# Another set of due times and engine choices for the jobs of an attention and gated-FFN kernel

## The chip, the cores and the metric

The program runs on one core of a Trainium2 chip. The metric is the device time of one execution in microseconds. Its engines have queues of their own: PE (TensorE: matmuls, with weight loads shown as PEld), DVE (VectorE), ACT (ScalarE), POOL (GpSimd) and SP (here only a queue that issues DMAs). Each queue runs strictly in the order in which its instructions were recorded, and an instruction waits on semaphores for what it reads or overwrites.

## The reference

Eight batches of eight heads, 576 positions, head size 64. Queries and keys are rotated, attention is computed per head, and the heads of a batch, laid side by side (512 channels), go through a gated block with a causal convolution of five taps.

```python
q_rot, k_rot = (rotate(q), rotate(k))
scores = scale * np.matmul(q_rot, k_rot.transpose(0, 1, 3, 2))
attn = np.exp(scores - max); attn = attn / (sum + 1e-09)
x = attn @ v                      # heads side by side: (8, 576, 512)
gate_pre += conv_w[k] * xp[:, k:k + S, :]          # k = 0..4
gate = 1.0 / (1.0 + np.exp(-gate_pre))
return gate * (x @ w_val) @ w_out
```

## The kernel before

The work is cut into 32 pairs of heads (p = 0 to 31), four pairs to a batch (b = 0 to 7). All products are float32 made of high and low parts (three products for one). The kernel records its work as some 3,400 jobs. A job has a name, a due time and an engine. The due time is a base written in the code plus an offset from the table DUE; the table PICK chooses the engine of the jobs that can run on more than one (V is DVE, A is ACT, G is POOL). `Plan.order` takes, of the jobs whose inputs were recorded and whose buffers are free, always the one with the smallest due time; this gives the order in every queue and also the rotation of the buffers. No due time is a time on the chip.

```python
            e = PICK.get(pick, e)
        plan.add(base + DUE.get(key, 0.0), e, fn, *args, r=r, w=w, port=port)
        heap = [(jobs[i][0], i) for i in range(len(jobs)) if not left[i]]
            i = heappop(heap)[1]
```

The jobs of one pair, with their names (a trailing e marks pairs 0 to 2, a trailing l the last pair or batch; `_0` and `_1` are the two column halves in which pair 0 is loaded and rotated):

- loadk, loadq, loadv: DMAs from SP (L198, L202). kmul0, kmul1, kadd, khi, klo and the same with q: the rotation and the split into high and low (L212, L216, L223, L227), on DVE, POOL and ACT. kfront and qmixed: small casts inside k, and of the last 64 query rows into a mixed tile (qm; L190 on ACT, L192 on DVE).
- s0 to s4: the scores (L255) of 128 query rows of both heads, s4 of the last 64 rows of both. They go to three PSUM banks. max0 to max8: row maxima on DVE (L261). exp0 to exp8: exponentials on ACT (L274), two to a score chunk; an exponential frees its bank.
- The probabilities are transposed. Pairs 3 to 30: x1, x3, x5, x7 turn 32x32 blocks on DVE (L289) and mv, 16 DMAs from SP (L294), put the blocks in place. Pairs 0 to 2 and 31: t0 to t7 and th on PE (L303, L316), with copies c0 to c7, ch1 and ch3 out of PSUM. tm, thm, cm, chm do this for the mixed rows.
- radd, rinv, rw, rr: reciprocal sums, written to DRAM and read back spread out. pv4, pv0, pv1: attention times v on PE (L359 to L377). norm0, norm1: DVE (L405).
- xhi, xlo: split of x (ACT L412, POOL L416). tap0 on ACT (L426), tap1 to tap4 on DVE (L429), gate on ACT (L433).

A batch whose four pairs are ready gives eight stage-0 groups f00 to f07 (four channel blocks by two column halves, 12 matmuls each, L463), each followed by a multiplication by the gate on DVE (L468), a high part on ACT (yh, L472) and a low part on POOL (yl, L476). Eight stage-1 groups f10 to f17 read these, go out through a copy on ACT or DVE (L482 on ACT) and a DMA from SP (L488). The groups of a batch lie between the scores of the pairs that come two to six places after its last one, in a pattern that repeats every four pairs.

The two weight matrices and the tap weights arrive as bits of 64-bit numbers. They are decoded in the head of the program: lval and lout load blocks (512 KB each, L527), dval and dout are six steps a block on DVE and ACT (L497 to L504), a cast (L534), a product on PE (L539 to L541) and a copy; dtap decodes the taps in seven instructions of 128x20 on DVE (L497 to L508). warm jobs are matmuls whose results nobody reads.

A POOL job that is recorded after a two-input DVE job waits for that DVE job by an added dependency (`self.behind`).

Of the kernel before, what the change touches and what calls it, by code (L numbers as in the profile page):

```python
# [144 lines left out]
def attn_gated_ffn(ctx: ExitStack, tc: tile.TileContext, q2, k2, v2, tab, w_val, conv_w, w_out, out, collect=None):  # L145
# [410 lines left out]
    def at(key, base, e, ns, fn, *args, pick=None, r="", w="", kb=0, mode=None, port=False):  # L556

        options = ns if pick else None
        if pick:
            e = PICK.get(pick, e)  # L560
            ns, port = options[e]
            args = [ENG[e] if a == "ENGINE" else a for a in args]
        plan.add(base + DUE.get(key, 0.0), e, fn, *args, r=r, w=w, port=port)
        if collect is not None:
# [244 lines left out]
```

## Time and profile before

| what | value |
|---|---|
| median of 3 runs | 650.75 us (646.76 to 650.79) |
| profiled execution | 650.38 us, its span 648.5 us |
| mean granted TensorE clock | 0.974 of full |
| busy, PE / DVE / ACT / POOL | 611.0 / 571.2 / 463.6 / 404.6 us |
| DMA | 139.16 MB, mean 215 GB/s |

The span is the time from the first to the last instruction; the execution has 1.9 us more around it. A busy PE counts matmuls at whatever clock was granted. The profile shows each instruction with the line of the kernel that recorded it, and the idle time before it with what ended it.

### The profile page before, as it was taken

The numbers are of one execution on the slowest core, as the hardware profiler recorded it, in microseconds if no ns is written. First come the engines' busy times: TensorE is split into PE (matmuls) and PEld (weight loads), VectorE is DVE, ScalarE is ACT, GpSimd is POOL, SyncE is SP. The second block draws the span as 40 slices with busy tenths as digits, with TensorE's granted clock in tenths as the row PEclk, the third lists the DMA queues.
The fourth block names the chain that finished last, engine by engine and source line by source line (L and its number), as shares of the span: only waits on it lengthen the run. The fifth ranks groups of instructions, "written<-read, shape, count | busy, mean of one in ns | idle before, by whom it ended". The sixth has DMA issues, their size and how long they took to land.

```text
span 648.5 us, 15339 instructions
## 1 busy us (share of the span) xinstructions
PE 611.0 (94%) x5611; PEld 500.6 (77%) x5611; DVE 571.2 (88%) x819; ACT 463.6 (71%) x1145; POOL 404.6 (62%) x309
## 2 busy tenths in 40 slices
PE   8898786899999999999999999999999999999997
PEld 8665554588878887888778887788788878888797
DVE  4999988899999999999999999999999998994532
ACT  3887866767777777876877777777877687776432
POOL 3324566678687869777778868776877777630200
PEclk9899976889999999999999999999999998999999
DMA  6634227888899899998999989999999889774011
GB/s 221 243 108 165 81 95 190 234 232 235 249 264 277 241 266 261 249 271 222 261 264 264 259 239 270 252 255 260 253 268 264 226 244 275 203 182 114 29 56 47
DMA packets 53019, 139.16 MB, mean 215 GB/s; under 512 B 11440, under 2 KB 21456, under 8 KB 52944
## 3 DMA queue, kind: packets, MB, share of 16 engines
q1 hardware_dynamic: 52400, 137.58, 75.4%
q8 instruction: 45, 0.74, 0.5%
q10 hardware_dynamic: 544, 0.59, 0.3%
q14 instruction: 30, 0.25, 0.1%
HBM read 62.48 MB, written 9.59 MB: 111 GB/s over the span
## 4 chain that ended last, share of the span: by engine, by line
PE 65%; DVE 11%; DMA 7%; POOL 5%; ACT 4%; issue 3%; SPq 3%; ACTq 0%; DVEq 0%; POOLq 0%
PE ps_t L463 23%; PE ps_s L255 16%; PE ps_t L369 14%; DVE nm L261 4%; DMA big<-big 3%; DVE big L289 3%; SPq L294 3%; PE ps_t L359 3%; PE ps_t L303 2%; DMA iq<-in_q 2%; PE ps_t L374 2%; DMA v<-in_v 2%; ACT p L274 2%; PE ps_t L330 2%; POOL yl L476 2%
## 5 line engine op out<-in xcount | busy, mean ns | idle before, releaser
L261 DVE TENSOR_REDUCE nm<-ps_s 128x1 f32<-128x576 f32 x288 | 204.6, 746 | 24.0 <-PE ps_s L255 23.8
L274 ACT ACTIVATE p<-ps_s,nm 128x576 f32<-128x576 f32 x256 | 188.3, 739 | 47.5 <-DVE nm L261 46.0
L255 PE MATMUL ps_s<-k,q 64*128 64x288 f32 x1536 | 146.9, 317 | 13.3 <-ACT p L274 9.7
L289 DVE STREAM_TRANSPOSE big<-p 128x1152 f32<-128x1152 f32 x112 | 150.9, 1361 | 0.0
L255 PEld LDWEIGHTS ps_s<-k,q 64*128 64x128 f32 x1536 | 112.7, 190 | 38.9 <-ACT p L274 19.9
L369 PE MATMUL ps_t<-big,v 128*64 128x256 f32 (+2 forms) x1024 | 119.4, 385 | 0.0
L429 DVE SCALAR_TENSOR_TENSOR g<-x,cw,g 128x576 f32<-128x576 f32 (+1 forms) x132 | 111.0, 843 | 1.5 <-ACT g L426 1.2
L212 POOL TENSOR_TENSOR iq<-iq,tab 128x576 f32<-128x576 f32 (+1 forms) x61 | 86.4, 1436 | 40.9 <-DVE g L429 8.9
L369 PEld LDWEIGHTS ps_t<-big,v 128*64 128x64 f32 x1024 | 70.8, 138 | 46.3 <-issue 15.6
L463 PE MATMUL ps_t<-yl,wout_hi 128*128 128x288 f32 x256 | 77.3, 302 | 4.9 <-POOL yl L476 4.9
L463 PE MATMUL ps_t<-xh,wval_hi 128*128 128x288 f32 x256 | 79.4, 310 | 0.0
L463 PE MATMUL ps_t<-yh,wout_hi 128*128 128x288 f32 x256 | 79.3, 310 | 0.0
L476 POOL TENSOR_TENSOR yl<-g,yh 128x288 fp32r<-128x288 f32 x56 | 48.8, 872 | 48.2 <-ACT yh L472 48.2
L227 POOL TENSOR_TENSOR q<-iq,q 128x576 fp32r<-128x576 f32 (+2 forms) x33 | 56.9, 1725 | 34.5 <-ACT q L223 30.6
L463 PE MATMUL ps_t<-xl,wval_hi 128*128 128x288 f32 x256 | 76.5, 299 | 0.0
L463 PE MATMUL ps_t<-xh,wval_lo 128*128 128x288 f32 x256 | 75.9, 296 | 0.0
L463 PE MATMUL ps_t<-yh,wout_lo 128*128 128x288 f32 x256 | 75.7, 296 | 0.0
L216 POOL TENSOR_TENSOR iq<-iq 128x576 f32<-128x576 f32 (+1 forms) x30 | 41.7, 1388 | 49.5 <-DVE g L429 43.2
L416 POOL TENSOR_TENSOR xl<-x,xh 128x576 fp32r<-128x576 f32 (+1 forms) x33 | 46.7, 1415 | 29.3 <-ACT xh L412 12.4
L463 PEld LDWEIGHTS ps_t<-yl,wout_hi 128*128 128x128 f32 x256 | 48.5, 189 | 7.3 <-POOL yl L476 6.3
L227 POOL TENSOR_TENSOR k<-ik,k 128x576 fp32r<-128x576 f32 x29 | 41.5, 1430 | 17.0 <-ACT k L223 5.3
L463 PEld LDWEIGHTS ps_t<-xh,wval_hi 128*128 128x128 f32 x256 | 49.3, 193 | 2.8 <-issue 2.6
(94 smaller groups left out, 1068.1 us busy)
## 6 DMA issues: line engine op xcount, KB each, us to landing
big<-big SPq DMA_DIRECT2D x448, 144.0 KB
ik<-in_k SPq DMA_DIRECT2D x31, 576.0 KB
iq<-in_q SPq DMA_DIRECT2D x31, 576.0 KB
v<-in_v SPq DMA_DIRECT2D x32, 320.0 KB
rb<-rd SPq DMA_DIRECT2D x64, 144.0 KB
out_t<-oo SPq DMA_DIRECT2D x64, 144.0 KB
big<-in_w_val SPq DMA_DIRECT2D x4, 512.0 KB
big<-in_w_out SPq DMA_DIRECT2D x4, 512.0 KB
```

Source lines behind the costliest of these rows:

```text
L212: eng.tensor_tensor(out=t[:, i, a:b], in0=t[:, i, a:b], in1=tabs[:, i, a:b], op=ALU.mult)
L216: eng.tensor_tensor(out=t[:, 0], in0=t[:, 0], in1=t[:, 1], op=ALU.add)
L227: eng.tensor_tensor(out=t[:, 1], in0=state[p][n + "in"][:, 0, a:b], in1=t[:, 0].bitcast(F32), op=ALU.subtract)
L255: T.matmul(out=ps[:, half, 0:288], lhsT=st["q"][rows, x, c * 128:c * 128 + 128] if c < 4 else mixq[p % 2][:, x], rhs=st["k"][rows, y, k0:k ...
L261: V.tensor_reduce(out=st[f"nm{i}"], in_=st[f"s{i}"], axis=AX.XY, op=ALU.max, negate=True)
L274: A.activation(out=pd.rearrange("p (b x) -> p b x", b=2), in_=st[f"s{i}"], func=AF.Exp, bias=st[f"nm{i}"], scale=1.0, accum_out=sums[p % 2 ...
L289: V.transpose(out=t[:, :, cs.index(c)].rearrange("p b k i -> p k b i"), in_=st[f"p{c}"].rearrange("p h s -> p (h s)").rearrange("p (k b i) ...
L369: T.matmul(out=acc[HEAD[h], 0:n], lhsT=st["v"][:, j, h, :], rhs=st["pt"][:, :, c0:c1, 5 * place(p, 2 * c0 + h) + j].rearrange("p a c i -> ...
L416: eng.tensor_tensor(out=st["xl"][:, a:b], in0=xs[p % 2][:, 4 + a:4 + b], in1=st["xh"][:, a:b].bitcast(F32), op=ALU.subtract)
L429: V.scalar_tensor_tensor(out=g, in0=x_sb[:, a + k:b + k], scalar=w, in1=g, op0=ALU.mult, op1=ALU.add)
L463: T.matmul(out=acc[:, 0:n], lhsT=wt[w][:, kc, ds], rhs=mv, start=(kc == 0 and i == 0), stop=(kc == NCH - 1 and i == 2))
L476: eng.tensor_tensor(out=ffn[b, "l", dc, lo], in0=y, in1=ffn[b, "h", dc, lo].bitcast(F32), op=ALU.subtract)
```

## The change

Only the two tables change. All 267 offsets of DUE have other values, so the order moves in every queue; 17 entries of PICK name another engine. No job is added, removed or altered, and DMAs are the same in number and size.

```diff
-DUE = {'taps': -9055.1904, 'dtap': 20.813, 'warm0': -111.0282, 'ltab_1': -9993.2863,
+DUE = {'taps': -8955.8597, 'dtap': -84.1915, 'warm0': -295.132, 'ltab_1': -9988.1565,
...
-PICK = {'c0': 'A', 'c0e': 'A', 'c1': 'A', 'c1e': 'A', 'c2': 'A', 'c2e': 'A', 'c3': 'V',
+PICK = {'c0': 'A', 'c0e': 'A', 'c1': 'V', 'c1e': 'A', 'c2': 'A', 'c2e': 'A', 'c3': 'A',
...
```

The 17 entries: from V to A qmixede and c3; from A to V ch3e, c1, c5, od1l and od2l; from G to V kmul0e, kmul1_0, qadd_0, qlo_0 and qlo_1; from V to G kmul1e, kadd_1, klo_0, kmul1_1 and qmul0_1.

What this does, first on DVE at the first pair, from its first two row maxima on (nm is written by a maximum, qm by a qmixed cast, L192 without qm is a copy of ch or c, 128x512 instructions on big are weight decoding). Before:

```order
L261 TENSOR_REDUCE nm_243<-ps_s_206 128x1
L261 TENSOR_REDUCE nm_270<-ps_s_205 128x1
L192 COPY qm_73<-q_71 64x2x64 x2
L261 TENSOR_REDUCE nm_278<-ps_s_254 128x1
L212 TENSOR_TENSOR ik_195<-ik_195,tab 128x576
L497 TENSOR_SCALAR big_234<-big_234 128x512
L261 TENSOR_REDUCE nm_292<-ps_s_255 128x1
```

Now the same place of DVE:

```order
L261 TENSOR_REDUCE nm_255<-ps_s_224 128x1
L261 TENSOR_REDUCE nm_274<-ps_s_225 128x1
L212 TENSOR_TENSOR ik_215<-ik_215,tab 128x576
L261 TENSOR_REDUCE nm_287<-ps_s_259 128x1
L261 TENSOR_REDUCE nm_291<-ps_s_260 128x1
```

The casts have left DVE (they are on ACT), and nothing stands between the third and the fourth maximum. The seven decoding steps of the taps, which stood among the work of pair 1, now stand on DVE ahead of the first scores. On SP a 512 KB block of w_val now stands between the first two loads and the other two loads of pair 0.

Second, DVE where pair 3 passes to pair 4 (x is L289; L429 are taps). Before, from max7 of pair 3 to max1 of pair 4:

```order
L261 TENSOR_REDUCE nm_1129<-ps_s_1116 128x1
L261 TENSOR_REDUCE nm_1133<-ps_s_1115 128x1
L289 STREAM_TRANSPOSE big_1034<-p_1101 128x9x4x32
L289 STREAM_TRANSPOSE big_1034<-p_1131 128x9x4x32
L429 SCALAR_TENSOR_TENSOR g_1071<-x_84,cw,g_1071 128x576
L429 SCALAR_TENSOR_TENSOR g_851<-x_85,cw,g_851 128x576
L261 TENSOR_REDUCE nm_1169<-ps_s_1162 128x1
L429 SCALAR_TENSOR_TENSOR g_1071<-x_84,cw,g_1071 128x576
L261 TENSOR_REDUCE nm_1188<-ps_s_1171 128x1
L261 TENSOR_REDUCE nm_1197<-ps_s_1172 128x1
```

Now, from max6 of pair 3 to max1 of pair 4:

```order
L261 TENSOR_REDUCE nm_1130<-ps_s_1116 128x1
L261 TENSOR_REDUCE nm_1132<-ps_s_1117 128x1
L502 SCALAR_TENSOR_TENSOR big_739<-big_739 128x512
L289 STREAM_TRANSPOSE big_1036<-p_1100 128x9x4x32
L503 TENSOR_SCALAR big_739<-big_739 128x512
L289 STREAM_TRANSPOSE big_1036<-p_1134 128x9x4x32
L429 SCALAR_TENSOR_TENSOR g_931<-x_85,cw,g_931 128x576
L504 SCALAR_TENSOR_TENSOR wout_lo<-big_739 128x512
L429 SCALAR_TENSOR_TENSOR g_1111<-x_84,cw,g_1111 128x576 x2
L261 TENSOR_REDUCE nm_1186<-ps_s_1172 128x1
L261 TENSOR_REDUCE nm_1190<-ps_s_1165 128x1
L261 TENSOR_REDUCE nm_1203<-ps_s_1173 128x1
```

The last steps of the last weight block moved behind the maxima of pair 3, and max8 of pair 3 behind max0 of pair 4; on PE the product of that block moved from ahead of s4 of pair 3 to between s0 and s1 of pair 4.

Third, DVE in the repeating pattern, where f06 and f05 of batch 1 are multiplied by the gate (L468). Before:

```order
L468 SCALAR_TENSOR_TENSOR g_2177<-g_2177,ps_t_3261 128x288
L429 SCALAR_TENSOR_TENSOR g_3241<-x_84,cw,g_3241 128x576
L261 TENSOR_REDUCE nm_3302<-ps_s_3289 128x1
L261 TENSOR_REDUCE nm_3304<-ps_s_3288 128x1
L468 SCALAR_TENSOR_TENSOR g_1919<-g_1919,ps_t_3314 128x288
L289 STREAM_TRANSPOSE big_3274<-p_3254 128x9x4x32
L429 SCALAR_TENSOR_TENSOR g_3241<-x_84,cw,g_3241 128x576
```

Now:

```order
L468 SCALAR_TENSOR_TENSOR g_2162<-g_2162,ps_t_3250 128x288
L429 SCALAR_TENSOR_TENSOR g_3226<-x_84,cw,g_3226 128x576
L261 TENSOR_REDUCE nm_3327<-ps_s_3283 128x1
L261 TENSOR_REDUCE nm_3331<-ps_s_3284 128x1
L289 STREAM_TRANSPOSE big_3270<-p_3265 128x9x4x32
L468 SCALAR_TENSOR_TENSOR g_1904<-g_1904,ps_t_3310 128x288
L429 SCALAR_TENSOR_TENSOR g_3226<-x_84,cw,g_3226 128x576
```

The multiplication for f05 moved behind a turn; on ACT its high part moved behind the second exponential of the chunk and kfront, where it stood between the two exponentials. On POOL the order there is unchanged. Elsewhere in the repeating pattern max8 stands behind max0 of the next pair, pv1 ahead of pv0, loadv behind rr, and single groups f trade places with their neighbours. In the last batch the two column halves trade places, the first half is now done first.

## Rows read from the trace of the kernel before

**Rows 1.** Windows: length, busy us (count) of PE, PEld, DVE, ACT, POOL; clock, DMA, GB/s
```profile
0.00:14.00 14.00, 11.98 (x82) 11.44 (x83) 5.85 (x17) 4.53 (x8) 3.88 (x10) 1.00 0.72 254
14.00:128.00 114.00, 94.54 (x722) 65.37 (x722) 101.62 (x159) 83.97 (x199) 55.79 (x39) 0.88 0.49 154
104.00:118.00 14.00, 12.28 (x62) 9.33 (x66) 11.20 (x14) 9.26 (x24) 10.03 (x7) 0.50 0.86 247
128.00:575.00 447.00, 436.82 (x4222) 364.38 (x4224) 430.61 (x587) 343.50 (x864) 336.96 (x253) 0.99 0.91 251
575.00:612.00 37.00, 35.50 (x353) 27.57 (x350) 20.14 (x34) 20.46 (x49) 6.33 (x6) 1.00 0.41 106
```

**Rows 2.** Timeline of PE, start and length in us, idle before and its releaser: pairs 3 to 4
```profile
102.60 0.61 PE L255 MATMUL ps_s<-k,q 64*128 64x288 f32 x1 [3.53 <-ACT pm L274]
```

**Rows 3.** Timeline of DVE, pairs 3 to 5
```profile
96.95 2.63 DVE L289 STREAM_TRANSPOSE big<-p 128x1152 f32<-128x1152 f32 x2
...
100.93 0.75 DVE L261 TENSOR_REDUCE nm<-ps_s 128x1 f32<-128x576 f32 x1
...
102.32 1.41 DVE L261 TENSOR_REDUCE nm<-ps_s 128x1 f32<-128x576 f32 x2
...
109.31 1.42 DVE L261 TENSOR_REDUCE nm<-ps_s 128x1 f32<-128x576 f32 x2 [1.00 <-PE ps_s L255]
...
113.57 1.42 DVE L261 TENSOR_REDUCE nm<-ps_s 128x1 f32<-128x576 f32 x2 [1.55 <-PE ps_s L255]
...
123.36 0.49 DVE L405 TENSOR_TENSOR x<-ps_t,rb 128x320 f32<-128x320 f32 x1 [1.40 <-PE ps_t L377]
```

**Rows 4.** Timeline of DVE, pairs 0 to 2
```profile
15.67 1.67 DVE L192 CAST qm<-q 64x128 fp32r<-64x128 f32 x2
17.45 0.76 DVE L261 TENSOR_REDUCE nm<-ps_s 128x1 f32<-128x576 f32 x1
18.24 0.76 DVE L212 TENSOR_TENSOR ik<-ik,tab 128x576 f32<-128x576 f32 x1
...
32.09 0.45 DVE L192 CAST qm<-q 64x128 fp32r<-64x128 f32 x2
...
53.19 1.49 DVE L192 CAST qm<-q 64x128 fp32r<-64x128 f32 x1
```

**Rows 5.** DVE by line and form: count, busy us, mean ns
```profile
L192 DVE COPY big<-ps_t 128x256 f32<-128x256 f32 x5 | 2.1, 420 | 1.4 <-PE ps_t L316 1.4
...
L499 DVE SCALAR_TENSOR_TENSOR oo<-oo,oo 128x20 int32<-128x20 int32 x1 | 0.2, 168 | 0.0
```

**Rows 6.** Timeline of POOL at the cast of pair 2
```profile
53.18 1.42 POOL L212 TENSOR_TENSOR iq<-iq,tab 128x576 f32<-128x576 f32 x1 [6.00 <-DVE wval_lo L504]
```

**Rows 7.** Timeline of PE, the stalls in the pattern of batch 0 and batch 1
```profile
182.68 1.05 PE L255 MATMUL ps_s<-k,q 64*128 64x288 f32 x11 [0.60 <-ACT p L274]
...
252.54 1.05 PE L255 MATMUL ps_s<-k,q 64*128 64x288 f32 x11 [0.60 <-ACT p L274]
...
255.13 0.40 PE L463 MATMUL ps_t<-yl,wout_hi 128*128 128x288 f32 x1 [0.82 <-POOL yl L476]
```

**Rows 8.** Timeline of DVE, the same place
```profile
251.66 0.45 DVE L468 SCALAR_TENSOR_TENSOR g<-g,ps_t 128x288 f32<-128x288 f32 x1
252.03 1.37 DVE L289 STREAM_TRANSPOSE big<-p 128x1152 f32<-128x1152 f32 x1
253.32 1.10 DVE L429 SCALAR_TENSOR_TENSOR g<-x,cw,g 128x576 f32<-128x576 f32 x1
```

**Rows 9.** Timeline of ACT, the same place
```profile
252.38 0.43 ACT L472 CAST yh<-g 128x288 fp32r<-128x288 f32 x1
...
253.43 0.30 ACT L190 CAST k<-k 128x128 fp32r<-128x128 f32 x1
```

**Rows 10.** Timeline of POOL, the same place
```profile
252.38 1.43 POOL L416 TENSOR_TENSOR xl<-x,xh 128x576 fp32r<-128x576 f32 x1
253.76 1.32 POOL L476 TENSOR_TENSOR yl<-g,yh 128x288 fp32r<-128x288 f32 x1
```

More of the change, by code (lines that the diff above doesn't have):

```diff
@@ L36 @@
-PICK = {'c0': 'A', 'c0e': 'A', 'c1': 'A', 'c1e': 'A', 'c2': 'A', 'c2e': 'A', 'c3': 'V', 'c3e': 'A', 'c4': 'A', 'c4e': 'A', 'c5': 'A', 'c5e': 'A', 'c6': 'A', 'c6e': 'A', 'c7': 'V', 'c7e': 'V', 'ch0': 'A', 'ch0e': 'V', 'ch1': 'V', 'ch1e': 'V', 'chm': 'A', 'chme': 'A', 'cm': 'A', 'cme': 'A', 'kadd': 'G', 'kadd_0': 'V', 'kadd_1': 'V', 'kadde': 'V', 'kfront': 'A', 'kfronte': 'A', 'klo': 'G', 'klo_0': 'V', 'klo_1': 'V', 'kloe': 'V', 'kmul0': 'G', 'kmul0_0': 'V', 'kmul0_1': 'V', 'kmul0e': 'G', 'kmul1': 'V', 'kmul1_0': 'G', 'kmul1_1': 'V', 'kmul1e': 'V', 'od0': 'A', 'od0l': 'A', 'od1': 'A', 'od1l': 'A', 'od2': 'A', 'od2l': 'A', 'od3': 'A', 'od3l': 'A', 'qadd': 'G', 'qadd_0': 'G', 'qadd_1': 'V', 'qadde': 'V', 'qlo': 'G', 'qlo_0': 'G', 'qlo_1': 'G', 'qloe': 'G', 'qmixed': 'A', 'qmixede': 'V', 'qmul0': 'G', 'qmul0_0': 'V', 'qmul0_1': 'V', 'qmul0e': 'G', 'qmul1': 'G', 'qmul1_0': 'G', 'qmul1_1': 'V', 'qmul1e': 'V', 'xlo': 'G', 'xloe': 'G', 'xlol0': 'G', 'xlol1': 'G', 'ylo': 'G', 'ylol': 'V', 'ch3': 'V', 'ch3e': 'A', 'decout': 'A', 'decval': 'A', 'odma': 'SP', 'odmal': 'SP', 'loadk': 'SP', 'loadk_0': 'SP', 'loadk_1': 'SP', 'loadke': 'SP', 'loadq': 'SP', 'loadq_0': 'SP', 'loadq_1': 'SP', 'loadqe': 'SP', 'loadv': 'SP', 'loadve': 'SP', 'mv0': 'SP', 'mv1': 'SP', 'mv2': 'SP', 'mv3': 'SP', 'rr': 'SP', 'rre': 'SP', 'rw': 'SP', 'rwe': 'SP'}
@@ new lines @@
+PICK = {'c0': 'A', 'c0e': 'A', 'c1': 'V', 'c1e': 'A', 'c2': 'A', 'c2e': 'A', 'c3': 'A', 'c3e': 'A', 'c4': 'A', 'c4e': 'A', 'c5': 'V', 'c5e': 'A', 'c6': 'A', 'c6e': 'A', 'c7': 'V', 'c7e': 'V', 'ch0': 'A', 'ch0e': 'V', 'ch1': 'V', 'ch1e': 'V', 'chm': 'A', 'chme': 'A', 'cm': 'A', 'cme': 'A', 'kadd': 'G', 'kadd_0': 'V', 'kadd_1': 'G', 'kadde': 'V', 'kfront': 'A', 'kfronte': 'A', 'klo': 'G', 'klo_0': 'G', 'klo_1': 'V', 'kloe': 'V', 'kmul0': 'G', 'kmul0_0': 'V', 'kmul0_1': 'V', 'kmul0e': 'V', 'kmul1': 'V', 'kmul1_0': 'V', 'kmul1_1': 'G', 'kmul1e': 'G', 'od0': 'A', 'od0l': 'A', 'od1': 'A', 'od1l': 'V', 'od2': 'A', 'od2l': 'V', 'od3': 'A', 'od3l': 'A', 'qadd': 'G', 'qadd_0': 'V', 'qadd_1': 'V', 'qadde': 'V', 'qlo': 'G', 'qlo_0': 'V', 'qlo_1': 'V', 'qloe': 'G', 'qmixed': 'A', 'qmixede': 'A', 'qmul0': 'G', 'qmul0_0': 'V', 'qmul0_1': 'G', 'qmul0e': 'G', 'qmul1': 'G', 'qmul1_0': 'G', 'qmul1_1': 'V', 'qmul1e': 'V', 'xlo': 'G', 'xloe': 'G', 'xlol0': 'G', 'xlol1': 'G', 'ylo': 'G', 'ylol': 'V', 'ch3': 'V', 'ch3e': 'V', 'decout': 'A', 'decval': 'A', 'odma': 'SP', 'odmal': 'SP', 'loadk': 'SP', 'loadk_0': 'SP', 'loadk_1': 'SP', 'loadke': 'SP', 'loadq': 'SP', 'loadq_0': 'SP', 'loadq_1': 'SP', 'loadqe': 'SP', 'loadv': 'SP', 'loadve': 'SP', 'mv0': 'SP', 'mv1': 'SP', 'mv2': 'SP', 'mv3': 'SP', 'rr': 'SP', 'rre': 'SP', 'rw': 'SP', 'rwe': 'SP'}
```

2 lines of the change are left out of this document (1 added, 1 removed).

## The prediction

> **What bounds the kernel now.** I read the table of busy time by stage first [rows 1]. From 128 to 575 us PE is busy 436.82 of 447 us: there TensorE is the bound, and DVE, busy 430.61 us, stands close behind. The pattern comes back after 69.9 us (252.54 - 182.68), and PE's timeline has only two gaps in each of its six passages: 0.60 us before a score chunk, which waits for an exponential to free its bank, and 0.82 us inside group f16, which waits for a low part from POOL [rows 7]. Six times 1.42 us is 8.5 of the 10.2 us that PE is idle in this stage. Nothing that only rearranges other engines can gain more than that here.
>
> From 14 to 128 us it is the other way round. PE is idle for 19.5 of 114 us and runs at a mean clock of 0.88, while DVE is busy 101.62 us, or 0.89 of the time [rows 1]. DVE has the weight decoding beside its maxima there, so what is taken off DVE in this stretch counts nearly in full, and 12.4 us of waiting is the most that a better order alone can win. The worst place is where pair 3 passes to pair 4: PE waits 3.53 us for the exponential that frees a bank [rows 2], and from 104 to 118 us its granted clock is 0.50, the lower level of 1.2 GHz [rows 1]. DVE then waits three times for the slow PE, 1.00, 1.55 and 1.40 us [rows 3]. Before the end, from 575 to 612 us, PE is idle 1.5 us [rows 1].
>
> The sum is made against the profiled execution, 650.38 us (span 648.5 us and 1.9 us around it). It lies 0.4 us under the median of the three runs, so the two can be used alike.
>
> **The change part by part.**
>
> *DVE work in the head.* The qmixed casts leave DVE for ACT, which has 30 us free in the stretch [rows 1]. Those of pair 1 cost 0.45 us and the long one of pair 2 1.49 us [rows 4]: together 1.94 us. Those of pair 0 cost 1.67 us, but the maximum behind them started at 17.45 only because PE had then just finished its scores, so I count them at nothing; that cover is worth up to 1.67 us if the scores come earlier. The copy ch3 comes to DVE three times, at 0.42 us each [rows 5]: 1.26 us added. The seven steps of dtap, 0.17 us each [rows 5], leave the full stretch for the time before the first scores, when DVE is busy 5.85 of 14 us [rows 1]: 1.18 us less. kmul0 and kmul1 of pairs 1 and 2 only trade engines. In all 1.94 - 1.26 + 1.18 = 1.86 us less, times 0.89 is **-1.7 us**. Bounds: nothing (all of it turns into waiting) and -3.5 us (with pair 0's casts).
>
> The long cast ran for 1.49 us while a POOL multiplication started 0.01 us before it and took 1.42 us [rows 4, 6]; the short pair beside an idle POOL took 0.45 us. The Trainium skill (SBUF — State Buffer, section Who interferes with whom) says that a DVE cast in its two-port mode and a GpSimd instruction exclude each other for the whole instruction, and that ACT waits for neither. These rows agree. By that rule the cast's whole 1.49 us go, since on ACT nothing locks it out, and the term is -1.7 us; without it the wait could pass to DVE's next instruction, only 0.45 us of pair 2's cast would go, and the term would be (0.90 - 1.26 + 1.18) x 0.89 = -0.7 us.
>
> *The first pair.* DVE's multiplication of 0.76 us that stood ahead of the fourth maximum [rows 4] moves to a place where DVE waits for PE's scores: -0.8 us. Against it, the first scores, which start shortly before 14 us, stand behind the taps and behind a load order in which a 512 KB block comes before half of pair 0. At 254 GB/s [rows 1] that block is 2.1 us. The delayed halves are needed last, behind the rotation of the first ones, so I take most of the 2.1 us as hidden and add 0.3 us (bounds -0.4, one DVE instruction of the rotation, and +1.2, all seven taps). Net **-0.5 us**.
>
> *Pair 3 to pair 4.* Weight steps move behind pair 3's maxima, so s0 of pair 4 can start earlier. But s1 of pair 4 needs two banks, those of max8 of pair 3 and of max0 of pair 4 and their exponentials. Before, max8 ran at 100.93 and the second tap and max0 after it [rows 3]; now the tap and max0 stand ahead of max8. The same instructions lie ahead of the second bank in both orders, so s1 starts when it did: **0 us**. In the hole that this leaves stands one weight product of PE. Bounds: -3.5 us (the hole closes) and +1.4 us (the two maxima once more).
>
> *The repeating pattern.* PE's order is the same but for pv1 ahead of pv0 and neighbours among the f groups, with equal work between the waits; loadv behind rr has a whole pair's time, a quarter of the 69.9 us, before it is read, and I cost both at nothing. The one place that touches a stall is f05. Its multiplication started at 251.66, behind it the turn, which took 1.29 us to the next start [rows 8]. Now it is behind the turn: it starts at 252.95 and ends at 253.40. The high part followed it on ACT at 252.38 [rows 9]; now both exponentials and kfront come first, and kfront, which ended at 253.73 with the high part's 0.32 us ahead of it, ends at 253.41. So the high part runs from 253.41 to 253.84, and the low part starts at about 253.9 instead of 253.76, when POOL was done with xl [rows 10]. Nearly all of the delay was covered by POOL. Six times 0.15 us is **+0.9 us**; bounds 0 and the rival below. The 0.60 us stall stays, since the first of the two exponentials still follows xhi.
>
> *The tail.* Copies c1 and c5 to DVE, c3 to ACT, od1l and od2l to DVE, the other column half first. PE's queue holds the same matmuls, and 1.5 us of waits are all there is to win or to shift: **0 us**, bounds -1.5 and +1.5.
>
> Sum: 650.4 - 1.7 - 0.5 + 0 + 0.9 + 0 = 649.1, say **649 us**.
>
> **The rivals.**
>
> A, *the clock is kept in the head*. If the weight product between s0 and s1 of pair 4 ends PE's wait in time, the 14 us at clock 0.50 don't come, and DVE's three waits for a slow PE, 3.95 us, go: 649.1 - 3.95 = 645 us. With half of DVE's other waits of the stretch (12.4 - 3.95, halved, is 4.2) it would be 641 us. For it: PE has one more piece of work in that place and s0 earlier. Against it: the piece itself waits for weight steps that now stand behind two turns on DVE.
>
> B, *f05 is late on POOL*, slower than before. Its place is the low part that f16 reads; the price is the whole delay of the turn, 1.29 us, in each of six batches, 7.7 us instead of 0.9: 649.1 + 6.8 = 656 us. It decides from the point at which POOL, done with xl at 253.76, waits for the high part longer than a tenth or two. For it: three things were put ahead, and the tap of DVE that stands beside the low part shows both instructions lengthened, 1.10 and 1.32 us [rows 8, 10]. Against it: POOL's own queue covered almost all of the delay in the working above.
>
> C, *the head's savings turn into waits*: DVE gets done earlier and waits for PE or ACT instead, as it already does for 12.4 us. Then only the 0.9 us remain: 651.3 us.
>
> **How the numbers follow.** The forecast has a chance of 0.45, A 0.20, B 0.15, C 0.20. The range goes from 641 (A with the halved waits) to 656 us (B), and leaves about 2 in 10 outside. One per cent, 6.5 us, is about what a measurement of this kernel can tell from no change. Under 644.2 us lie half of A and what the bounds of the forecast allow, 0.19; over 657.3 us lies the upper part of B and a head with a second stretch at the lower clock, 0.11; 0.70 are left for a change within 1%.
>
> **What the profile after would show.** Two PE gaps in each passage of the pattern as before, the one in f16 between 0.8 and 1.1 us: right for the pattern. DVE busy about 99 to 100 us in the stretch that ends with the first f04, and that stretch shorter by 2 us: right for the head. PE's gap before s1 of pair 4 cut in two by a weight product, with a clock of 0.5 behind it: right for that place. It is wrong if the period of a batch, 69.9 us, has changed by more than 0.3 us, if the clock in the head stays at its upper level (2.4 GHz) or falls in other places for long, or if a transfer, most of all the early 512 KB block, ends a wait on the path.

## The result: 1.0% slower

The changed kernel takes 653.09 us (median of 12, 651.40 to 657.49), the kernel before 647.24 us in the same comparison (median of 12, 643.92 to 650.79). The ratio is 1.0101, 95% interval 1.0071 to 1.0131. Ratios leave out executions that took over 1.5% longer than the fastest of their kernel; in e15 below these are two of twelve, at 660 us. I had forecast 649 us from a profiled execution of 650.38 us, so 1.3 us faster; measured is 5.9 us slower. That 653 us still lies between 641 and 656 us is in part luck: the execution that I started from took 3.1 us more than the median of before here.

The profiled execution after has a span of 651.2 us (652.97 us in all). In that of before the fourth period has a wait for a transfer (70.86 instead of 69.86 us), the clock fell behind its last pattern stall (1.45 us, see the end), and 4.4 us lie behind its last matmul where other kernels with that end have 3.3 to 3.7. By stages, with these three (1.0, 1.45 and about 1.1 us) taken out: the first stall of the pattern came 0.7 us later, the five periods between the first stall and the last took 355.94 instead of 349.3 us (**+6.6 us**), and the rest 111.85 instead of 112.9 us (-1.1): +6.2 us, close to the measured +5.9.

The table by stage, after (columns as in [rows 1]):

```profile
0.00:14.00 14.00, 8.48 (x54) 8.24 (x55) 7.43 (x21) 3.99 (x7) 4.42 (x10) 0.89 0.82 291
14.00:128.00 114.00, 98.70 (x751) 68.48 (x749) 101.29 (x152) 84.93 (x203) 55.39 (x39) 0.87 0.50 153
104.00:118.00 14.00, 12.57 (x64) 8.76 (x64) 11.45 (x15) 8.73 (x24) 10.66 (x8) 0.50 0.78 226
128.00:575.00 447.00, 432.49 (x4181) 355.11 (x4182) 432.54 (x580) 331.92 (x855) 335.75 (x251) 0.99 0.93 249
575.00:612.00 37.00, 36.46 (x348) 29.82 (x346) 24.09 (x39) 22.20 (x55) 7.74 (x8) 1.00 0.46 123
```

Against [rows 1] PE did 4.2 us more work in the stretch from 14 to 128 us, but this is work that it had not done by 14 us: from 0 to 128 us both kernels do 803 matmuls. From 128 to 575 us it lost 4.3 us of work, and DVE became busier by 1.9 us. What holds PE up there is in its table of waits (us in total, times, longest):

```profile
PE ps_t L463 <- POOL yl L476: 4.9, 6, 0.8
PE ps_s L255 <- ACT p L274: 4.5, 7, 0.9
PE ps_t L345 <- DVE pm L386: 2.7, 9, 0.5
PE ps_t L359 <- DMA big<-big: 1.8, 3, 0.8
PE ps_t L359 <- DMA ik<-in_k: 0.6, 1, 0.6
```

The first two are the old stalls of [rows 7] and the last waits ahead of the pattern, nearly unchanged. The last three, 5.1 us, are new but for 0.4 us: thm waits for the reciprocal sums of DVE, and pv4 for moved blocks of the turned probabilities. Why DVE is late is seen where f03 and f07 of batch 2 are multiplied. Before, DVE and then POOL (idle time and releaser in brackets):

```profile
297.16 0.81 DVE L429 SCALAR_TENSOR_TENSOR g<-x,cw,g 128x576 f32<-128x576 f32 x1
```

```profile
293.64 0.81 POOL L476 TENSOR_TENSOR yl<-g,yh 128x288 fp32r<-128x288 f32 x1
295.21 1.42 POOL L216 TENSOR_TENSOR iq<-iq 128x576 f32<-128x576 f32 x1 [0.76 <-DVE g L429]
```

After, DVE, then POOL, then PE's first matmul behind it:

```profile
295.83 1.22 DVE L429 SCALAR_TENSOR_TENSOR g<-x,cw,g 128x576 f32<-128x576 f32 x1
296.97 2.07 DVE L261 TENSOR_REDUCE nm<-ps_s 128x1 f32<-128x576 f32 x3
298.97 1.48 DVE L429 SCALAR_TENSOR_TENSOR g<-x,cw,g 128x576 f32<-128x576 f32 x1
301.78 0.20 DVE L386 RECIPROCAL pm<-sums 128x9 f32<-128x9 f32 x1
```

```profile
296.40 2.07 POOL L476 TENSOR_TENSOR yl<-g,yh 128x288 fp32r<-128x288 f32 x2
298.43 1.41 POOL L216 TENSOR_TENSOR iq<-iq 128x576 f32<-128x576 f32 x1
...
310.04 1.43 POOL L212 TENSOR_TENSOR iq<-iq,tab 128x576 f32<-128x576 f32 x1 [2.62 <-DMA iq<-in_q]
```

```profile
302.12 0.30 PE L345 MATMUL ps_t<-ident,pm 128*128 128x128 f32 x1 [0.30 <-DVE pm L386]
```

qadd (298.43 to 299.84) was running when tap4 came at 298.97; the tap ended 0.61 us after qadd and took 1.48 us where this tap took 0.81 before. qadd was that late because two low parts (f03 and f07) stand ahead of it now, where before only f03 did; the section on the change doesn't name this trade. Three maxima beside the same POOL work took 2.07 us, as in e15 below. The reciprocal ends at 301.98, and PE has waited 0.30 us. The late qadd also delays qlo, and with it, so I read it, the buffer for the next q: POOL then waited 2.62 us for its load, 9.7 us in 9 such waits from 128 to 575 us (2.8 us in 2 before).

### The profile page after: what moved, and what is told of

The parts are those of the page before. It is cut to its first block, busy times and chain, and to the rows that moved or that the text cites. A ratio compares the mean times of both kernels' runs of the same rounds, so it can differ in the third digit from the quotient of the medians.

```text
span 651.2 us, 15347 instructions
## 1 busy us (share of the span) xinstructions
PE 612.0 (94%) x5611; PEld 495.6 (76%) x5611; DVE 581.2 (89%) x821; ACT 453.5 (70%) x1143; POOL 407.4 (63%) x309
## 4 chain that ended last, share of the span: by engine, by line
PE 60%; DVE 16%; DMA 11%; ACT 5%; issue 3%; SPq 3%; POOL 1%; DVEq 0%; ACTq 0%
PE ps_t L463 23%; PE ps_s L255 15%; PE ps_t L369 11%; DMA big<-big 7%; DVE nm L261 5%; DVE big L289 5%; DVE g L429 3%; DMA ik<-in_k 3%; PE ps_t L359 2%; SPq L294 2%; ACT p L274 2%; PE ps_t L303 2%; PE ps_t L330 2%; PE ps_t L374 1%; PE ps_t L439 1%
## 5 line engine op out<-in xcount | busy, mean ns | idle before, releaser
L289 DVE STREAM_TRANSPOSE big<-p 128x1152 f32<-128x1152 f32 x112 | 151.7, 1362 | 0.0
L255 PEld LDWEIGHTS ps_s<-k,q 64*128 64x128 f32 x1536 | 112.9, 190 | 46.0 <-ACT p L274 22.3
L429 DVE SCALAR_TENSOR_TENSOR g<-x,cw,g 128x576 f32<-128x576 f32 (+1 forms) x132 | 126.1, 956 | 0.4
L369 PE MATMUL ps_t<-big,v 128*64 128x256 f32 (+2 forms) x1024 | 124.6, 386 | 0.0
L212 POOL TENSOR_TENSOR iq<-iq,tab 128x576 f32<-128x576 f32 (+2 forms) x62 | 88.6, 1443 | 46.2 <-DMA iq<-in_q 14.2
L369 PEld LDWEIGHTS ps_t<-big,v 128*64 128x64 f32 x1024 | 68.4, 138 | 41.1 <-issue 14.7
L476 POOL TENSOR_TENSOR yl<-g,yh 128x288 fp32r<-128x288 f32 x56 | 54.7, 982 | 44.0 <-ACT yh L472 43.5
L227 POOL TENSOR_TENSOR q<-iq,q 128x576 fp32r<-128x576 f32 x31 | 48.7, 1571 | 44.3 <-ACT q L223 42.7
L416 POOL TENSOR_TENSOR xl<-x,xh 128x576 fp32r<-128x576 f32 (+1 forms) x33 | 48.9, 1482 | 37.6 <-ACT xh L412 19.6
L216 POOL TENSOR_TENSOR iq<-iq 128x576 f32<-128x576 f32 x29 | 40.9, 1409 | 28.4 <-DVE g L429 26.2
L227 POOL TENSOR_TENSOR k<-ik,k 128x576 fp32r<-128x576 f32 (+1 forms) x30 | 42.6, 1419 | 18.5 <-DVE g L429 9.7
L463 PEld LDWEIGHTS ps_t<-yh,wout_hi 128*128 128x128 f32 x256 | 48.7, 190 | 2.6 <-issue 1.3
```

The costliest lines, as they stand in the source:

```text
L212: eng.tensor_tensor(out=t[:, i, a:b], in0=t[:, i, a:b], in1=tabs[:, i, a:b], op=ALU.mult)
L216: eng.tensor_tensor(out=t[:, 0], in0=t[:, 0], in1=t[:, 1], op=ALU.add)
L227: eng.tensor_tensor(out=t[:, 1], in0=state[p][n + "in"][:, 0, a:b], in1=t[:, 0].bitcast(F32), op=ALU.subtract)
L255: T.matmul(out=ps[:, half, 0:288], lhsT=st["q"][rows, x, c * 128:c * 128 + 128] if c < 4 else mixq[p % 2][:, x], rhs=st["k"][rows, y, k0:k ...
L289: V.transpose(out=t[:, :, cs.index(c)].rearrange("p b k i -> p k b i"), in_=st[f"p{c}"].rearrange("p h s -> p (h s)").rearrange("p (k b i) ...
L369: T.matmul(out=acc[HEAD[h], 0:n], lhsT=st["v"][:, j, h, :], rhs=st["pt"][:, :, c0:c1, 5 * place(p, 2 * c0 + h) + j].rearrange("p a c i -> ...
```

## The experiments

All times are medians, all ratios are against the kernel before on the same chip, with 95% intervals. Where a table is edited, P are the 84 offsets of pairs 3 to 30 and of the groups of batches 0 to 6, H the 131 offsets of pairs 0 to 2, the weights and the start, L the 52 of the last pair and batch.

**Parts alone (e1, e2, e3, e11, e12, e18).** Each takes the named parts of both tables from the changed kernel, the rest stays as before:

```diff
 e1: P    e2, e11: H    e3: L    e12: H and P    e18: H and L
-DUE = {... the part, before ...}
+DUE = {... the part, after ...}
```

> Only the offsets of the pairs 3 to 30 and of the groups of batches 0 to 6 are those of the changed kernel; head and last batch keep the old ones. Theory 1 (the loss is in the repeating pattern: the six periods of the profile after are 71.2 instead of 69.9 us, +5.6 us in all): slower than before by 5 to 8 us, ratio 1.008 to 1.012, since the gain of 3.7 us behind the last pattern stall is not in it. Theory 2 (the head sets the pace, and the pattern only inherits a worse start): within 1.5 us of before.

> Only the offsets and engines of pairs 0 to 2 and of the decoding of the weights are those of the changed kernel. Theory 1: the trace after reaches the first pattern stall 0.7 us later than before, so +0.7 us (0 to +1.5), and the period is 69.9 us as before. Theory 2: slower by 4 us or more, with longer periods although the pattern is the old one.

> Only the offsets and engines of the last pair and the last batch are those of the changed kernel. Theory 1: the part behind the last pattern stall, 111.85 instead of 115.5 us, shortens by up to 3.7 us: between -3.7 and 0 against before. Rival (that shorter end is only the other side of a longer pattern, work done already while the pattern waited): within 1 us of before.

> The kernel with only the head of the changed kernel, once more, for a profile (its 11 timed executions gave 653.7 us, 6 us over before). If the head itself is slow, the first stall of the pattern comes at 186 to 189 us instead of 182.7. If it comes within 1 us of 182.7, the loss lies behind it, in the pattern or at the end, though their orders are those of before.

> The changed kernel with the old order in the last pair and the last batch. If the shorter end of the changed kernel (111.9 against 115.5 us behind the last stall) comes from its own last batch, this is slower than the changed kernel by 3 to 8 us (119.7 us was measured there with the new pattern and the old end): 656 to 661 us. If the end follows from the pattern, it is the same as the changed kernel, 653 us.

> Head and last batch of the changed kernel with the old pattern. If the losses of the parts add up, head alone (+6 us) and last batch alone (+7 us) make it 13 us slower than before: 660 us, and the changed pattern, which then brings 653 us, is a gain beside these two. If the pattern is the loss of the change, this is 3 us or less slower than before.

| kernel | us | ratio |
|---|---|---|
| e1 P | 666.46 | 1.0284 (1.0226 to 1.0342) |
| e2 H | 653.67 | 1.0092 (1.0058 to 1.0127) |
| e3 L | 655.01 | 1.0087 (1.0051 to 1.0123) |
| e12 H, P | 659.49 | 1.0192 (1.0159 to 1.0226) |
| e18 H, L | 659.63 | 1.0171 (1.0126 to 1.0216) |
| after: H, P, L | 653.09 | 1.0101 (1.0071 to 1.0131) |

None of the parts is free. H and L add up (0.9 and 0.9 against 1.7% in e18), P does not: the three single losses make 4.6%, the whole loses 1.0%. The last batch costs 0.9% beside the old pattern and gives 0.9% back beside the new one (1.0192 to 1.0101). e1 lost 18.8 us, far over the 5 to 8 us expected; its pattern took 357.29 us between its first and last stall, as theory 1 says (8.0 us more), and the rest lies ahead of it and behind it. By parts the answer differs from that by stages: beside the changed head and last batch, the changed pattern is a gain of 0.7 points (1.0171 to 1.0101), as the expectation of e18 says for that result. It loses its 6.6 us between the stalls, but with the old pattern the first stall came at 188.34 instead of 183.41 us and the rest behind the last stall took 118.4 instead of 111.85 us. So "the pattern is the loss" holds for the stage and not for the part. e11 is e2 once more, for its trace: 653.27 us, first stall at 185.09 us, 2.4 us later than in [rows 7]; of the five periods behind it, two were at the old 69.86 us, in two the clock fell, and the last took 70.57.

**The taps' order alone (e4).**

```diff
-'kmul1': 18.3059, 'tap4': 36.7731, 'norm0': 26.8498, 'norm1': 25.9637,
+'kmul1': 17.6557, 'tap4': 35.5325, 'norm0': 19.9937, 'norm1': 3.084,
 (and x1 to x7, vz, pv, xhi, tap0 to tap3 and gate as after)
```

> In the pattern only the offsets of taps, gate, norms, turns, xhi and kmul1 are those of the changed kernel (maxima, exponentials, POOL, SP and groups as before). On DVE the last tap now stands ahead of kmul1 and the norms of the older pair trade places. Theory 1a (the taps now meet POOL's instructions, both lengthened, and DVE, already busy 430.61 of 447 us, becomes the bound): the mean tap grows from 864 towards 956 ns and the time by 3 to 7 us. Rival 1b (the maxima and exponentials are the cause: max8 behind max0 of the next pair delays radd and rinv): within 1.5 us of before. Rival 1c (loads and moves from SP land late): within 1.5 us of before.

704.55 us, 1.0855 (1.0797 to 1.0912), far over the 3 to 7 us expected. In this mix tap4 follows the first maximum directly. DVE, then POOL, in one pair:

```profile
257.00 0.75 DVE L261 TENSOR_REDUCE nm<-ps_s 128x1 f32<-128x576 f32 x1
257.67 1.60 DVE L429 SCALAR_TENSOR_TENSOR g<-x,cw,g 128x576 f32<-128x576 f32 x1
```

```profile
257.23 1.42 POOL L216 TENSOR_TENSOR iq<-iq 128x576 f32<-128x576 f32 x1 [3.21 <-DVE g L429]
```

The tap ended at 259.27, 0.62 us after qadd's end at 258.65. Over pairs 8 to 27 tap4 took 1.66 us on average, against 0.81 before. This shows the mechanism at its largest, not its share in the change: in this mix pv1 and pv0 also trade places on PE, and the stall in f16 grew from 0.82 to 3.1 us.

**max8 moved, or put back (e5, e6, e9, e13).**

```diff
 e6, on before (e5: the reverse, on after)
-'max8': 5.1487, 'exp8': 13.5046, 'radd': -23.9491, 'tap4': 36.7731, 'kmul1': 18.3059,
+'max8': 23.0492, 'exp8': -10.0676, 'radd': 9.4714, 'tap4': 35.5325, 'kmul1': 17.6557,
 (and max0, max1, tap3, norm0, norm1, rinv)
 e9 and e13, on after: as e5 without rinv, and
-'norm0': 19.9937, 'norm1': 3.084,
+'norm0': 26.85, 'norm1': 25.6,   (e13: 25.7, and 'tap4': 36.3)
```

> The changed kernel with one place of DVE put back in every pair from 3 on: max8 again ahead of tap3 and kmul1 ahead of tap4 (order x7, max8, tap3, max0, max1, kmul1, tap4); POOL, SP and the groups stay as changed. Theory 1a (without max8 between x7 and tap3 the tap meets the multiplication of q that POOL is in, and waits until it has ended; tap4 meets qadd): tap3 falls from 1157 to about 910 ns, tap4 from 1004 to about 805, kmul1 rises from 745 to about 930, net 0.26 us a pair, 1.0 us a batch: period 70.2 instead of 71.2 us, time 647 us (645 to 650). Rival 1c (late loads and moves of SP, which stay): 653 us as the changed kernel.

> The kernel before with that one place of DVE alone changed: x7, tap3, max0, max8, max1, tap4, kmul1 (exp8 and radd follow max8 on ACT); POOL's and SP's orders stay. Theory 1a: taps 3 and 4 lengthen as in the changed kernel, less what POOL's own order did (the f07 low part ahead of qadd): 0.15 to 0.3 us a pair, the period 70.5 to 71.1 us, the time 651 to 656 us. Rival 1c: 647.6 us as before.

> The changed kernel with max8 again ahead of tap3 and kmul1 ahead of tap4, as in the earlier run of that idea, but now with everything on PE as in the changed kernel (thm stays ahead of f06) and the norms in the order in which PE delivers (norm1 before norm0; norm1 between kmul1 and tap4). That earlier run was slow (665 us): its norm0 stood ahead of norm1 while PE does pv1 first, and DVE stood still 0.4 us before it in most pairs. Theory 2a (the loss of that run is this mismatch; the tap's place itself helps): taps 3 and 4 and kmul1 together as before the change (2646 ns against 2906), period 70.0 to 70.6 us, time 647 to 651 us. Rival 2b (max8 ahead of tap3 does harm in the changed order): 660 us or more. Rival 2c (only POOL's order matters): 653 us.

> The changed kernel with max8 ahead of tap3 and kmul1 ahead of tap4, now with norm1, norm0 and rinv behind tap4 and nothing moved on PE, POOL or SP. Theory 3a (who starts first decides: max8's place keeps tap3 out of the multiplications of q, and tap4 starts before qlo): tap3 falls from 1157 to about 950 ns, tap4 from 1004 to 805 to 900, kmul1 rises to about 1000; about 0.1 us a pair less, period 70.7 to 71.0 us, time 650 to 653 us. Rival 3b (max8 ahead of tap3 harms in the changed order whatever the norms do): 660 us or more.

e5 took 665.48 us, 1.0238 (1.0181 to 1.0295); e6 655.82, 1.0110 (1.0060 to 1.0159); e9 667.73, 1.0317 (1.0282 to 1.0352); e13 658.51, 1.0133 (1.0078 to 1.0188). e6 was in its band for the wrong reason: its period was 70.14 us, only 0.28 us over the old one, and most of its loss lay ahead of the pattern. Of the three attempts to put max8 back e5 and e9 were slower than the changed kernel, and e13 was no faster (the intervals overlap). The first two had a fault of mine. In e5, thm had also slipped behind f06 on PE, and norm0 stood ahead of norm1 although PE delivers pv1 first. In e9 norm1 stood between kmul1 and tap4, and that was enough. DVE and POOL of e9:

```profile
264.39 0.92 DVE L212 TENSOR_TENSOR ik<-ik,tab 128x576 f32<-128x576 f32 x1
265.24 0.48 DVE L405 TENSOR_TENSOR x<-ps_t,rb 128x320 f32<-128x320 f32 x1
265.64 1.87 DVE L429 SCALAR_TENSOR_TENSOR g<-x,cw,g 128x576 f32<-128x576 f32 x1
```

```profile
265.48 1.42 POOL L227 TENSOR_TENSOR q<-iq,q 128x576 fp32r<-128x576 f32 x1 [0.78 <-ACT q L223]
```

qlo began 0.16 us ahead of tap4, so the tap waited it out (1.87 us) and qlo took its 1.42. In the old order tap4 is first and qlo waits: tap4 0.81, qlo 1.84 us on average. Who starts first decides who pays. The Trainium skill (SBUF — State Buffer, section Who interferes with whom) says so too: the order of issue decides which of the two blocks; the two cases agree with that. e13 had neither fault, and rival 3b was the nearer one: max8 ahead of tap3 does not repair the time of the changed order. That the removed max8 lengthens tap3 is true (1157 against 910 ns), and its share is seen in the undisturbed period of each kernel, from stall to stall, with no fall of the clock and no wait for a transfer (e7, e15, e14 and e17 follow below):

| kernel | undisturbed period, us |
|---|---|
| before; e17 (before, f07 moved) | 69.86; 69.85 |
| e6 (before, max8 moved) | 70.14 |
| after | 70.42 |
| e13 (after, max8 back) | 70.20 |
| e15; e7 (after, POOL's order back) | 70.09; 70.08 |
| e14 (after, both back) | 69.82 |

The place of max8 (with the taps, kmul1 and norms that move with it) is worth 0.22 to 0.28 us a period in three settings (before to e6, e13 to after, e14 to e7). Why e13 is no faster all the same is not shown: in its trace one period took 73.23 us, with PE waits of 1.50 us for moved blocks and 1.03 us for the reciprocal, the first stall came 1.7 us later than in the changed kernel, and the clock fell behind three of its stalls.

**POOL's order put back (e7, e15, e10, e14, e17).**

```diff
 e15, on after (e17: the reverse, on before)
-'f07': 21.4556,
+'f07': 22.2267,
 e7: also
-'qmul0': 9.9053, 'qmul1': 5.2481,
+'qmul0': 6.0535, 'qmul1': 5.3104,
 e10: e9 and e7 together    e14: e13 and e7 together
```

> The changed kernel with POOL's order partly put back: qmul0 ahead of qmul1, and the low part of f07 behind qadd and qlo; DVE's order stays as changed. Theory 1a: tap4 of every fourth pair, 1.48 us, falls to about 0.8, since qadd then starts at the end of tap3 and is over before tap4; tap3 of the pair two further (1.6 us) stays, since a multiplication of q still runs there. 0.7 us a batch: period 70.5 us, time 649 us (648 to 651). Rival 1c: 653 us. Rival 1d (max8 behind max0 costs by the later exponential, not by POOL): 653 us.

> The changed kernel with only the low part of f07 put back behind qadd and qlo on POOL (f07's other steps move by a neighbour on ACT). Theory 3a: tap4 of every fourth pair, 1.48 us, falls to about 0.8: 0.7 us a batch, period 70.5 us, time 649 to 651 us, and no more than that is left for the order of the two multiplications of q. If that order carries it: 653 us.

> Both repairs on the changed kernel: max8, taps and norms as in the run above, and POOL's order as in the earlier run with qmul0 ahead of qmul1 and the low part of f07 behind qlo. If DVE's lengthened instructions are the whole loss of the pattern, the period is back at 69.9 us; against the run with POOL's part alone (period 70.55 us) that is 3 to 4 us less: 647 to 649 us, within 1 us of before or faster. If a part of the loss lies elsewhere (the order of SP, or the groups), it stays at 650 to 652 us.

> The same with POOL's order back too (qmul0 ahead of qmul1, the low part of f07 behind qlo). Theory 3a: the lengthened instructions of a pair come to about 4.45 us as before the change (4.41), the period to 69.9 to 70.1 us; the head stays as changed (0 to 2 us longer) and the end too (3.7 us shorter, if it depends on the pattern's length and not on max8): 645 to 649 us. Rival 3b: 660 us.

> The kernel before with the low part of f07 alone moved ahead of qadd on POOL (and f07's high part by one neighbour on ACT). In the old order kmul1, not tap4, follows the two maxima behind tap3, and max8 lies ahead of tap3. Theory 3a: qadd starts up to 0.8 us later, so that kmul1 and tap4 of every fourth pair meet it; 0.2 to 0.7 us a batch, of which the slack of DVE beside PE covers a part: 0 to 4 us slower than before, tap4 of that pair over 0.9 us or kmul1 over 1.1 us. If it harms only beside the changed taps: within 1.5 us of before.

e7: 651.85 us, 1.0049 (1.0011 to 1.0087). e15: 650.86 us, 1.0037 (1.0006 to 1.0068). The one offset of f07 thus takes 0.64 points of the 1.01% away. The interval of e15 just misses that of the changed kernel (1.0068 against 1.0071), that of e7, which has the same edit, overlaps it. The traces say the same: the five periods of e15 took 353.9 us, with one fall of the clock (1.45 us) in them, against 355.9. The multiplications of q add nothing that shows. The orders of PE and DVE are the same in after and e15; the offset moves f07's low part on POOL and, on ACT, its high part behind the step radd on the sums (L383). ACT isn't the cause: in after it stood idle for 1.18 us behind that high part and one small copy. The same place in e15:

```profile
296.15 1.22 DVE L429 SCALAR_TENSOR_TENSOR g<-x,cw,g 128x576 f32<-128x576 f32 x1
297.30 2.07 DVE L261 TENSOR_REDUCE nm<-ps_s 128x1 f32<-128x576 f32 x3
299.30 0.80 DVE L429 SCALAR_TENSOR_TENSOR g<-x,cw,g 128x576 f32<-128x576 f32 x1
301.55 0.20 DVE L386 RECIPROCAL pm<-sums 128x9 f32<-128x9 f32 x1
302.18 1.42 DVE L261 TENSOR_REDUCE nm<-ps_s 128x1 f32<-128x576 f32 x2 [0.43 <-PE ps_s L255]
```

```profile
297.99 1.42 POOL L216 TENSOR_TENSOR iq<-iq 128x576 f32<-128x576 f32 x1
```

qadd now runs beside the maxima and is over at 299.41, when tap4 has hardly begun: 0.80 us. DVE is early and waits for PE. POOL's waits for q are 2.4 us in 3, PE's for the reciprocal 0.4 us in 2. The second period, undisturbed in all three, is 70.09 instead of 70.42 us, and 69.86 before (windows from stall to stall; e15, after, before):

```profile
254.99:325.08 70.09, 68.47 (x668) 56.27 (x668) 68.43 (x93) 52.78 (x137) 53.39 (x41) 1.00 0.94 253
```

```profile
254.66:325.08 70.42, 68.46 (x668) 56.27 (x668) 68.77 (x93) 52.77 (x137) 53.73 (x41) 1.00 0.92 249
```

```profile
252.54:322.40 69.86, 68.45 (x668) 57.01 (x668) 67.56 (x93) 54.12 (x137) 53.47 (x41) 1.00 0.90 251
```

PE's work is the same to 0.02 us. From e15 to after DVE's is 0.34 us longer, and the period 0.33: tap4 is longer by 0.68 us, the tap behind it shorter by 0.32. From before to e15 DVE's grew by 0.87 us and the period by 0.23: there DVE still had idle time to give. The undisturbed period explains 2.8 of the 6.6 us (5 x 0.56); the other periods of the changed kernel, 70.57 to 72.37 us, are longer by 3.8 us in all. Three of these four hold the waits of PE for transfers in the table above, 2.4 us; why those come late is not shown.

e17 puts the same two neighbours into the kernel before: 647.87 us, 1.0000 (0.9963 to 1.0038). There kmul1 of every fourth pair met qadd (1.38 to 1.39 instead of 0.92 us), but the tap that follows it got shorter by 0.28, so that DVE's busy time in an undisturbed period grew by only 0.1 us (67.64 against 67.54), and the period stayed at 69.85 us. So the same trade on POOL cost nothing in the old order, where it mostly shifted a wait from one DVE instruction to another. e10 (664.15 us, 1.0272, 1.0231 to 1.0314) carries the fault of e9. e14 (655.52 us, 1.0111, 1.0077 to 1.0144) had one undisturbed period of 69.82 us, as theory 3a said, but pv4 waited three times for transfers, 0.57 to 1.10 us, and its end was longer than that of the changed kernel (114.3 against 111.85 us, of which a fall of the clock is 1.45): the time is not repaired.

**SP's order, and the norms (e16, e8).**

```diff
 e16, on before
-'loadq': -66.2281, 'loadv': 18.552, 'rw': 12.9121, 'rr': 28.2878,
+'loadq': -39.3487, 'loadv': 20.8538, 'rw': 24.0807, 'rr': 29.5264,
 (and loadk, mv0 to mv3)
 e8, on before
-'norm0': 26.8498, 'norm1': 25.9637,
+'norm0': 18.35, 'norm1': 18.36,
```

> The kernel before with SP's order alone moved in the pattern (offsets of loadk, loadq, loadv, rw, rr and the moves). Theory 3a: no DVE, POOL, ACT or PE order changes, so within 1.5 us of before (647.6 us). Rival 1c (loads and moves land later and hold PE up at pv4 or POOL at the multiplications of q): 2 to 6 us slower, with waits for a transfer of 2 us or more in the pattern on PE.

> The kernel before with norm0 and norm1 moved ahead of kmul1 and tap4 on DVE (x7, max8, tap3, max0, max1, norm0, norm1, kmul1, tap4, rinv). Theory 1a: kmul1 no longer starts while qadd runs, 931 to 745 ns, 0.19 us a pair off DVE. PE has only 1.42 us of idle time a batch, so the gain is between 0 and 4 us; a norm that has to wait for PE, as 14 of them did before, would give part of it back: 644 to 649 us. Rival 1e (DVE has so much slack in the pattern that a few tenths a pair don't count): 647.6 us, no change.

e16: 649.61 us, 1.0024 (0.9991 to 1.0058). Rival 1c (2 to 6 us) did not come, but the interval leaves room for up to 0.58%, and PE waited once for a transfer, 1.16 us. e8: 683.57 us, 1.0551 (1.0493 to 1.0610), where I expected 644 to 649 us. Its waits, DVE's and PE's:

```profile
DVE x L405 <- PE ps_t L377: 38.7, 24, 1.8
```

```profile
PE ps_t L345 <- DVE pm L386: 33.2, 24, 1.7
```

The norms came 1.6 us (38.7 us in 24 waits) ahead of PE's products and held up the reciprocal behind them, for which PE then waited 33.2 us in all.

No version beats the kernel before.

## Why the prediction was wrong

**The step that failed** is the repeating pattern. I wrote that the one place that touches a stall is f05, costed everything else at nothing and put +0.9 us there. Measured: +6.6 us between the first stall and the last, of which 2.8 us are the undisturbed period (70.42 instead of 69.86 us) and the rest single longer periods, and f05 itself cost nothing. Two of my signs contradicted each other here: the gap in f16 between 0.8 and 1.1 us came and was to mean "right for the pattern", while the period moved by 0.56 us, over the 0.3 that was to mean "wrong". The first sign only watched the chain that I had worked out. The stall in f16 is 0.82 us as before, since the low part began 1.34 us after the score chunk (1.22 us in [rows 7, 10]) but took 1.20 instead of 1.32 us. PE, ACT and POOL at that place:

```profile
254.66 1.05 PE L255 MATMUL ps_s<-k,q 64*128 64x288 f32 x11 [0.59 <-ACT p L274]
257.25 0.40 PE L463 MATMUL ps_t<-yl,wout_hi 128*128 128x288 f32 x1 [0.82 <-POOL yl L476]
```

```profile
255.49 0.43 ACT L472 CAST yh<-g 128x288 fp32r<-128x288 f32 x1
```

```profile
256.00 1.20 POOL L476 TENSOR_TENSOR yl<-g,yh 128x288 fp32r<-128x288 f32 x1
```

So I followed the one chain whose order moved ahead of a known stall, and did not ask what the neighbours on POOL that traded places would meet on DVE. My own rows held the mechanism ([rows 4, 6]: the cast held up by a multiplication of POOL), I used it for one cast in the head and not here. By e15, 0.64 of the 1.01 points are the low part of f07 ahead of qadd; it is shown by one offset. The remaining 0.37 points are not taken apart by times. In the undisturbed period what is left in e15 (0.23 us) goes with the place of max8: taps of about 1.6 us are still there in two of four pairs, and e14 is back at 69.82 us. The longer single periods and the later start stay open; SP's order alone, on before, was not told from no change. A rival that no run tests: the executions of the changed kernel show a lower mean clock (0.968, against 0.975 in the 92 of before beside the experiments), and what this costs is not separated.

**DVE work in the head (-1.7).** DVE was busy 101.29 us from 14 to 128 us, not 99 to 100. The casts went (3.8 us), but two taps and two decoding steps (L499) now started while POOL was in an instruction, and took 1.74, 1.87, 1.90 and 1.62 us, where before no tap of this stretch took over 0.91 and no such step over 0.69: about 4 us more. This is the step that failed in the pattern once again: what POOL was doing when a DVE instruction began had no term in the sum. My working had a wait that passes to DVE's next instruction only as the other case, at -0.7 us. The two taps on DVE, then POOL beside them:

```profile
56.36 3.64 DVE L429 SCALAR_TENSOR_TENSOR g<-x,cw,g 128x576 f32<-128x576 f32 x2
```

```profile
56.07 3.32 POOL L212 TENSOR_TENSOR iq<-iq,tab 128x576 f32<-128x576 f32 x2 [4.17 <-DMA iq<-in_q]
```

All the same the stretch from the first scores to PE's last wait for a bank ahead of the pattern became 4.7 us shorter: it began 4.5 us later (below) and ended at 129.15 instead of 129.32 us. How much of that is the better order, and how much is work that DVE had done ahead of the late scores, is not shown. Between 129 us and the first stall 0.9 us were lost again. My lower bound of -3.5 us left out the factor 0.89; with it, it is -3.1.

**The first pair (-0.5)** was mis-sized by 5 us. The first scores started 4.5 us later, and the maxima behind them at 18.66 instead of 14.11 us (PE before, then after):

```profile
12.83 1.07 PE L255 MATMUL ps_s<-k,q 64*128 64x288 f32 x12
```

```profile
12.14 5.28 PE L439 MATMUL ps_t<-q 128*128 128x256 f32 x23 [4.16 <-ACT q L223]
17.34 1.29 PE L255 MATMUL ps_s<-k,q 64*128 64x288 f32 x12
```

My upper bound was +1.2 us for all seven steps of the taps. They took DVE from 8.79 to 11.31 us, 2.5 us, ahead of the addition that q waits for. Ahead of them, ACT waited 3.82 us for the rotation table to land, where before it waited 1.00: the sign of a transfer that ends a wait on the path, which I had named. PE waited 4.16 us, and its mean clock from 0 to 14 us was 0.89. How the delay divides between taps and loads is not shown.

**Pair 3 to 4 (0)** held: the wait was cut up by the weight product, as foretold, and s1 began at 102.16 instead of 102.60 us.

```profile
94.50 0.40 PE L255 MATMUL ps_s<-k,q 64*128 64x288 f32 x1 [1.91 <-ACT p L274]
95.22 1.05 PE L255 MATMUL ps_s<-k,q 64*128 64x288 f32 x11 [0.32 <-ACT p L274]
99.05 0.79 PE L540 MATMUL ps_t<-wout_lo,minus 128*128 128x512 f32 x1 [2.00 <-DVE wout_lo L504]
...
102.16 2.53 PE L255 MATMUL ps_s<-k,q 64*128 64x288 f32 x12 [0.61 <-ACT p L274]
```

PE idles here for 2.2 us ahead of s0, 2.0 inside the product and 0.6 ahead of s1, in all 4.8 us; before it was 3.53 [rows 2] and 0.79 more inside s1. The clock from 104 to 118 us is 0.50 as in [rows 1]; **rival A** did not come, for the reason given against it, that the product itself waits for DVE. **Rival B** did not come (0.82 us). **Rival C** named a loss of the head's savings and gave 651.3 us, near the result by luck: the head did not lose what it saved to waits alone, and the pattern lost 6.6 us, not 0.9. **The tail (0)**: -1.1 us beside the new pattern, inside its bounds, but +0.9% beside the old (e3), where 0 to 3.7 us faster was expected. In its table of waits e3 has PE waiting for the copies of the turned blocks, 5.5 us, where before had 1.3; why is not shown.

## What to carry to other kernels

When an order moves, list for each two-input DVE instruction which POOL instruction runs at its start, before and after; a neighbour that trades places on POOL is not free if that list changes. Here the trade made DVE 0.34 us longer a period in the changed order, and the period with it (e15 to after); in the old order it made DVE 0.1 us longer and cost nothing (e17). Parts of one schedule need not be additive terms: the pattern alone lost 2.8%, and beside the other two parts it gained 0.7 points. A test by parts tells which parts fit together; a single exchanged pair, read in the undisturbed period and not only in the total time, tells a cause. Put one offset back first.

## What the hardware showed unexpectedly

Behind the two old stalls (0.60 us and, 2 us later, 0.82 us) PE's granted clock sometimes fell to 0.50, its lower level of 1.2 GHz, for about 3 us, and sometimes not, in the same program: 18 of 84 passages in the profiles of 14 kernels (those that have both stalls at these lengths). Where nothing else disturbed the period behind such a fall, it was longer by 1.4 to 1.5 us. Two periods of e11, whose order is the same, and the stretch behind the first stall:

```profile
185.09:256.44 71.35, 69.94 (x668) 58.49 (x668) 67.53 (x93) 54.22 (x137) 53.42 (x41) 0.98 0.94 256
...
327.76:397.62 69.86, 68.46 (x668) 57.00 (x668) 67.55 (x93) 54.11 (x137) 53.47 (x41) 1.00 0.95 263
```

```profile
187.60:190.60 3.00, 2.92 (x12) 2.93 (x13) 3.00 (x4) 2.71 (x7) 3.00 (x4) 0.50 0.96 264
```

PE's busy time grew by 1.48 us with the same 668 matmuls. Six passages at 1.45 us could spread the executions of one kernel by up to 8.7 us (an estimate); among 92 executions of before those with a mean clock of 0.981 took 644.4 us on average, those with 0.966 took 651.8. A span read from one profile was no measure of the change: here it told +2.7 us where the medians tell +5.9.
